# First pair's decay rows made in SBUF, small routing work of early batches on GpSimd, and a new table of planner weights in an attention + MoE + MLP kernel

## The chip, the cores and the metric

One core of one Trainium2 chip runs the whole program. Its engines are TensorE (PE in the profile, with its weight loads apart as PEld), VectorE (DVE), ScalarE (ACT), GpSimd (POOL) and SyncE (SP), which here only issues DMAs. The metric is the device time of one execution in microseconds; lower is better.

## The reference, cut to what matters

```python
def _attn_ref(q, k, v, f):                 # (4, 8, 576, 64), f (4, 8, 576)
    scores = scale * np.matmul(q, k.transpose(0, 1, 3, 2))
    cum = np.cumsum(np.log(np.clip(f, 0.0001, 1.0)), axis=-1)
    decay = cum[:, :, :, None] - cum[:, :, None, :]
    scores = np.where(causal, -1000000000.0, scores + decay)
    scores = scores - np.max(scores, axis=-1, keepdims=True)
    attn = np.exp(scores)
    attn = attn / (np.sum(attn, axis=-1, keepdims=True) + 1e-09)
    return np.matmul(attn, v)

def _moe_ref(x, w_gate, w_output_gate, w1, w2):   # x (2304, 512), 8 experts
    logits = x @ w_gate
    e_idx = np.argmax(logits, axis=1)
    probs = softmax(logits); gate_w = probs[np.arange(N), e_idx]
    eom = 1.0 / (1.0 + np.exp(-(x @ w_output_gate)))
    out[mask] = gate_w[mask, None] * eom[mask, e, None] * (np.maximum(x[mask] @ w1[e], 0) @ w2[e])

def _moe2_ref(x, w_in, w_out, a, b):              # a rational activation between two matmuls
    h = x @ w_in
    g = (a0 + a1*h + a2*h**2 + a3*h**3) / (1 + |b0|*|h| + |b1|*h**2 + 1e-06)
    return g @ w_out
```

## The kernel before, in words

The program has four stages: attention with its routing (0 to about 200 us), the token routing (to about 216 us), the experts (to about 480 us) and the last MLP. The change is in the first two.

Attention works on 16 pairs of heads (`pair(p)`, four pairs to a batch of 576 tokens). For one pair, K and Q come by DMA (`rk`, `rq`) and are split into a high and a low float32r part: `kh` (a cast on VectorE) and `qs` (ScalarE), then `kl`, the low half of `qs`, and a copy `q2s`. These three run on GpSimd for pairs 1 to 15 and on VectorE for pair 0. `kls` and `q2s` also hold two spare rows per head: `q2s` has ones there, and `kls` the cumulated log decay of the keys (a high and a low part), so that the second of the two score matmuls (L457) adds the decay. `kls`, `q2s` and `qs` have two buffers each, blanked by memsets at the start.

The decay itself is made once for all 32 heads at the start: `f` is loaded to 32 partitions, clipped, put through Ln, summed by a scan, split into high (`f_high`, L329) and low (`f_low`, L333), and stored to a scratch tensor `cum_d` in DRAM (L338, two DMAs). Each pair's `load_c` (L388) reads its four rows from there into `kls`.

A pair's scores are then taken in seven steps (the tiles of 128 queries, some for both heads at once). A step is two score matmuls per head (L456 and L457; L467 and L468 for the last 64 queries of both heads), a masked minimum on VectorE (`least`, L479 and L491), the exponential on ScalarE (L511, L522), transposes on TensorE (L598, L578, L582), and the copy of the transposed weights out of PSUM (`move`, L291 on ScalarE or L293 on VectorE). When a pair's weights are there, PV (L621) follows, and its result is copied to `ot`.

After a batch's four pairs, `batch(b)` routes its tokens: the sums of the weights (`tails`, `swap`, `tails2`, `norm`), logits from `ot` (`logit`, `tr`, `scale`), the choice of the expert (`choose`), its gate (`gates_a`, `gates_x`, `gates_b`), and the token rows scaled by the factor `rg` and stored to `x_d` (`rows_t`, `rows_m`, `rows_d`). All of the small tensors there (128 x 4 to 128 x 40) are worked on by VectorE, save two activations. The last batch's choice and gates are written out behind the plan, as part of the token routing, since the next stage waits for them.

The order of everything in attention is set by a planner (`Plan`): each operation has a due time (`when`), an engine or two with a length, and what it needs, takes and frees. A list scheduler goes through them by engine and emits the instructions in that order, and no scheduler changes it afterwards (`manual_schedule`). The due times are built from one table of weights:

```python
T_STEP = (0.003, 0.167, 0.576, 1.046, 0.372, 0.855, 1.261)
...
T_BATCH, T_BATCHJ, T_ROWS = 0.299, 0.239, -5.772
```

What goes to GpSimd before the plan (the memsets, masks, constants) stands in program order with the compiler's scheduler. 80 idle matmuls (`idle`, L353) run on TensorE at the start while it has no work.

Of the kernel before, what the change touches and what calls it, by code (L numbers as in the profile page):

```python
# [21 lines left out]
P = 128  # L22
BIG = 1.0e30
# [114 lines left out]
def tile_attention_moe_mlp(  # L138
# [37 lines left out]
    nc.scalar.preload_act_table_set("natural_log_exp_and_others")  # L176

# [11 lines left out]

    identf = const.tile([P, P], F32, name="identf")  # L190
    make_identity(nc, identf)
# [20 lines left out]
    pref = ec.tile([P, NE], F32, name="pref")  # L212
    nc.gpsimd.iota(pref, pattern=[[-1, NE]], base=NE, channel_multiplier=0, allow_small_or_imprecise_dtypes=True)

    prefs = ec.tile([P, NI, NE], F32, name="prefs")
    nc.gpsimd.tensor_copy(prefs, pref.unsqueeze(1).to_broadcast([P, NI, NE]))
    nc.gpsimd.memset(prefs[TL:, NQ], 0.0)


    with ExitStack() as actx, ExitStack() as rctx:  # L220
# [8 lines left out]

        qs = [wk.tile([P, 2, S + P], F32R, name=f"qs{i}", bufs=1) for i in range(2)]  # L230
        for t in qs:
            nc.gpsimd.memset(t.bitcast(F32)[:, :, S:], 0.0)
        half = (slice(0, D), slice(D, P))
# [5 lines left out]
        for t, k in zip(q2s, kls):  # L239
            nc.gpsimd.memset(t.bitcast(F32), 0.0)  # L240
            nc.gpsimd.memset(k.bitcast(F32), 0.0)
            for h in range(2):
                nc.gpsimd.memset(t.bitcast(F32)[half[1 - h].start : half[1 - h].start + 2, h, 0:S], 1.0)
# [5 lines left out]
        mask = wk.tile([P, NQ * P], F32, name="mask", bufs=1)  # L249
        mask_t = wk.tile([P, S // 2], F32, name="mask_t", bufs=1)  # L250
        nc.gpsimd.memset(mask, 0.0)
        nc.gpsimd.memset(mask_t, 0.0)
        for t in [mask[:, (NQ - 1) * P :]] + [mask_t[h * TL : (h + 1) * TL, S // 2 - TL :] for h in range(2)]:
            nc.gpsimd.affine_select(
                out=t, in_=t, compare_op=ALU.is_ge, fill=BIG / SCALE, base=0, pattern=[[-1, t.shape[-1]]], channel_multiplier=1
            )
# [9 lines left out]
        T_STEP = (0.003, 0.167, 0.576, 1.046, 0.372, 0.855, 1.261)  # L266
        T_TRANS = (0.59, 0.851, 0.237, 0.235, -3.102, 0.47, -0.137)
# [29 lines left out]


        g0 = {}

        def f_load(e):
            g0["fl"] = wt("t")[:NBH]
            nc.sync.dma_start(out=g0["fl"], in_=f)
# [584 lines left out]
        with tc.manual_schedule():  # L888
            plan.emit()
# [761 lines left out]
```

## Time and profile before

| | us |
|---|---|
| three timed runs | 888.17, 889.30, 893.38 |
| median | 889.3 |
| the profiled execution | 889.93 |
| its span in the trace | 888.2 |

Over the span PE is busy 849.3 us (96%), DVE 747.9 (84%), ACT 615.6 (69%) and POOL 337.5 (38%). PE's busy time is that of pipelined matmuls, and its ends are modelled: a full PE means that it always had a matmul under way. The gap of 1.7 us between the profiled execution and its span lies ahead of and behind what the trace covers. In a timeline each line is the start, the length, the engine, the line of the kernel, the operation and tiles, and in brackets how long the engine had been idle and what ended that; in a group, the busy time and the mean length in ns stand behind the first bar.

### The profile page before, as it was taken

The page shows a single profiled execution, that of the slowest core. Times are in us where ns is not written, and L with a number is a line of the kernel's source. Part 1 is how long each engine was busy: PE and PEld are TensorE (multiplying, and loading weights), DVE is VectorE, ACT ScalarE, POOL GpSimd, SP SyncE. Part 2 cuts the span into 40 slices and gives each one's busy share as a digit, 9 for nine tenths or more (in the row PEclk, how much of TensorE's full clock was granted, in tenths as well). Part 3 has the DMA queues.
Part 4 walks back from the last instruction along what each step waited for, and adds up shares of the span by engine and source line. Part 5 has one row for each costly group of instructions (what it writes and reads, how often), then busy time and mean ns, then how long its engine had stood idle before and what let it go on. Part 6 is the DMA issues. An engine that isn't in the chain of part 4 may idle for free. (4 is left out here: it accounts for less than half of the span.)

```text
span 888.2 us, 15292 instructions
## 1 busy us (share of the span) xinstructions
PE 849.3 (96%) x4667; PEld 705.0 (79%) x4667; DVE 747.9 (84%) x1428; ACT 615.6 (69%) x1282; POOL 337.5 (38%) x364
## 2 busy tenths in 40 slices
PE   6999898996999999999999999999999999999997
PEld 6787786764888887888787788899888889988885
DVE  7798999778798878778876999898898878988882
ACT  4889897876465667567545878777676667777772
POOL 7888586502113232223241233343233224324222
PEclk9999999997999999999999999999999999999999
DMA  6776567604866588789564121010000001000001
GB/s 167 167 182 168 154 175 212 199 27 151 298 218 217 177 263 310 226 288 316 195 218 154 48 72 37 0 60 24 13 36 25 12 1 57 16 1 36 1 0 48
DMA packets 49130, 110.32 MB, mean 124 GB/s; under 512 B 8405, under 2 KB 12526, under 8 KB 49038
## 3 DMA queue, kind: packets, MB, share of 16 engines
q1 hardware_dynamic: 36910, 69.90, 26.4%
q0 software_dynamic: 12128, 39.34, 13.3%
q8 instruction: 40, 0.66, 0.3%
q14 instruction: 52, 0.43, 0.2%
HBM read 151.79 MB, written 20.35 MB: 194 GB/s over the span
## 5 line engine op out<-in xcount | busy, mean ns | idle before, releaser
L1519 POOL TENSOR_TENSOR gl<-raw,gh 128x512 fp32r<-128x512 f32 (+1 forms) x71 | 84.2, 1186 | 207.3 <-ACT gh L1517 127.2
L1535 PE MATMUL pa<-wu,gl 128*128 128x512 f32 x256 | 100.6, 393 | 1.1 <-POOL gl L1519 1.1
L1533 PE MATMUL pa<-wu,gh 128*128 128x512 f32 x256 | 101.2, 395 | 0.0
L1534 PE MATMUL pa<-wu,gh 128*128 128x512 f32 x256 | 100.1, 391 | 0.0
L1492 ACT ACTIVATE raw<-ph 128x512 f32<-128x512 f32 (+1 forms) x80 | 44.3, 554 | 78.1 <-PE ph L1484 74.8
L1058 DVE TENSOR_TENSOR wu<-raw,wu 128x1024 fp32r<-128x1024 f32 x64 | 75.2, 1219 | 8.0 <-ACT wu L1056 6.6
L511 ACT ACTIVATE pr<-t,mn 128x384 f32<-128x384 f32 (+3 forms) x128 | 70.7, 557 | 16.0 <-DVE mn L479 15.4
L1505 DVE SCALAR_TENSOR_TENSOR raw<-raw,coef,raw 128x512 f32<-128x512 f32 (+1 forms) x80 | 66.2, 827 | 17.8 <-ACT raw L1501 15.1
L1495 DVE SCALAR_TENSOR_TENSOR raw<-raw,babs 128x512 f32<-128x512 f32 (+1 forms) x80 | 58.3, 729 | 20.9 <-ACT raw L1493 20.2
L1482 PE MATMUL ph<-colAh,wi 128*128 128x512 f32 x192 | 74.9, 390 | 1.0 <-ACTq L1423 0.7
L1484 PE MATMUL ph<-colAh,wi 128*128 128x512 f32 x192 | 74.7, 389 | 0.0
L1483 PE MATMUL ph<-colAl,wi 128*128 128x512 f32 x192 | 74.7, 389 | 0.0
L1056 ACT ACTIVATE wu<-raw 128x1024 fp32r<-128x1024 f32 x64 | 63.8, 1066 | 4.1 <-DMA raw<-in_w_dram 2.2
L479 DVE CUSTOM_DVE_ANT_0 t<-s,mask 128x384 f32<-128x384 f32 (+3 forms) x128 | 57.8, 484 | 6.5 <-PE s L457 3.0
L1506 DVE SCALAR_TENSOR_TENSOR raw<-raw,cbias 128x512 f32<-128x512 f32 (+1 forms) x80 | 57.6, 720 | 2.3
L1500 ACT ACTIVATE raw<-raw,cbias 128x512 f32<-128x512 f32 (+1 forms) x80 | 55.0, 687 | 6.3 <-DVE raw L1495 5.8
L1494 ACT ACTIVATE raw<-ph,neg 128x512 f32<-128x512 f32 (+1 forms) x80 | 59.3, 741 | 0.0
L1535 PEld LDWEIGHTS pa<-wu,gl 128*128 128x128 f32 x256 | 48.0, 188 | 12.7 <-POOL gl L1519 2.4
L1497 DVE SCALAR_TENSOR_TENSOR raw<-raw,coef,ph 128x512 f32<-128x512 f32 (+1 forms) x80 | 55.5, 694 | 2.5
L1533 PEld LDWEIGHTS pa<-wu,gh 128*128 128x128 f32 x256 | 48.1, 188 | 9.5 <-ACT gh L1517 0.7
L1534 PEld LDWEIGHTS pa<-wu,gh 128*128 128x128 f32 x256 | 48.1, 188 | 9.0
L1507 DVE SCALAR_TENSOR_TENSOR raw<-raw,raw 128x512 f32<-128x512 f32 (+1 forms) x80 | 52.4, 655 | 2.4
(263 smaller groups left out, 2391.9 us busy)
## 6 DMA issues: line engine op xcount, KB each, us to landing
raw<-in_w_dram SPq DMA_DIRECT2D x92, 1024.0 KB
rk<-in_kT_dram SPq DMA_DIRECT2D x30, 288.0 KB
rq<-in_qT_dram SPq DMA_DIRECT2D x30, 288.0 KB
d<-in_w_in_dram POOLq DMA_DIRECT2D x16, 512.0 KB
d<-in_w_out_dram POOLq DMA_DIRECT2D x16, 512.0 KB
y_d<-ys SPq DMA_DIRECT2D x22, 256.0 KB
v<-in_v_dram SPq DMA_DIRECT2D x16, 256.0 KB
wo_d<-d POOLq DMA_DIRECT2D x16, 256.0 KB
```

The lines of the kernel that those rows point to most:

```text
L511: nc.scalar.activation(u["pr"][:, sl], u["t"][:, sl], AF.Exp, bias=u["mn"][:, m : m + 1], scale=-1.0, accum_out=sm[:, i, 2 * hp + h : 2 * ...
L1056: nc.scalar.activation(w[:, 0], r, AF.Copy)
L1058: nc.vector.tensor_tensor(w[:, 1], r, w[:, 0].bitcast(F32), ALU.subtract)
L1482: nc.tensor.matmul(out_, wh, hi[:, :, c], start=(c == 0), stop=False)
L1483: nc.tensor.matmul(out_, wh, lo[:, :, c], start=False, stop=False)
L1484: nc.tensor.matmul(out_, wl_, hi[:, :, c], start=False, stop=(c == KD - 1))
L1494: nc.scalar.activation(u_, ph, AF.Identity, scale=neg[:, 3:4], bias=neg[:, 2:3])
L1505: nc.vector.scalar_tensor_tensor(u_, u_, coef[:, 0:1], rr, ALU.subtract, ALU.mult)
L1519: low.tensor_tensor(d["gl"], d["u_"], d["gh"].bitcast(F32), ALU.subtract)
L1533: nc.tensor.matmul(a_, gh[:, sl], wh, start=(m == 0), stop=False)
L1534: nc.tensor.matmul(a_, gh[:, sl], wl_, start=False, stop=False)
L1535: nc.tensor.matmul(a_, gl[:, sl], wh, start=False, stop=(m == MF - 1))
```

## The change

- The first pair's two decay rows per head are made in SBUF. `f` is loaded to 66 partitions, so that the first batch's heads 0 and 1 also lie on the partitions that pair 0's `kls` needs; clip, Ln, scan and `f_high` work on 66 partitions, with a column `sgn` as the factor, and `f_rows` writes the rows straight to `kls` (two operations of 2 x 576 on VectorE). Pair 0's `load_c` is gone. The other pairs still read `cum_d`; its two stores and the 32-row `f_low` are due later. The loads of `f` are three DMAs (two on SyncE's queue, one on ScalarE's), and the activation table is preloaded behind ScalarE's.
- Pair 0's second `kh` and its two `q2s` copies go from VectorE to ScalarE, and its `kls` memset from GpSimd to VectorE. The memsets and masks are reordered, with what pair 0 needs first; `identf`, `pref` and `prefs` come later, and the loads of `coef` are planned into SyncE's queue behind the second pair.
- In batches 0 to 2, the sums, products and differences of small tensors whose operands are all in SBUF go to GpSimd (12 operations a batch: `tt`, `sums`, `ex`, `gs`, `den`, `oz`, `rg`), and each is planned as an operation of its own. Reductions, reciprocals and what reads PSUM stay on VectorE. The choice takes the first maximum from the difference `ex` in one operation in place of two. The last batch uses the same functions on VectorE.
- The table of weights is new throughout.

```diff
-    nc.scalar.preload_act_table_set("natural_log_exp_and_others")
...
+    sgn = ec.tile([P, 2], F32, name="sgn")
+    nc.vector.memset(sgn, 1.0 / SCALE)
+    for r in (0, D):
+        nc.vector.memset(sgn[r : r + 1, 0:1], -1.0 / SCALE)
+        nc.vector.memset(sgn[r : r + 1, 1:2], 0.0)
...
+
+        def blank(i, on):
+            t = q2s[i].bitcast(F32)
+            on.memset(kls[i].bitcast(F32), 0.0)
+            nc.gpsimd.memset(t, 0.0)
             for h in range(2):
-                nc.gpsimd.memset(t.bitcast(F32)[half[1 - h].start : half[1 - h].start + 2, h, 0:S], 1.0)
+                nc.gpsimd.memset(t[half[1 - h].start : half[1 - h].start + 2, h, 0:S], 1.0)
+            nc.gpsimd.memset(qs[i].bitcast(F32)[:, :, S:], 0.0)
+
+        blank(0, nc.vector)
...
+        T_STEP = (-0.667, 0.087, 0.246, 0.842, 0.232, 0.882, 0.93)
...
+        T_BATCH, T_BATCHJ, T_ROWS = 0.558, 0.17, 1.464
...
+            g0["fl"] = wt("t")
+            nc.scalar.dma_start(out=g0["fl"][D:NF], in_=f[0:1, :].to_broadcast([2, S]))
+            nc.sync.dma_start(out=g0["fl"][F0], in_=f)
+            nc.sync.dma_start(out=g0["fl"][0:NBH], in_=f[1:2, :].to_broadcast([NBH, S]))
+            nc.scalar.preload_act_table_set("natural_log_exp_and_others")
...
         def f_high(e):
-            g0["ch"] = wt("pr")[:NBH].bitcast(F32R)
-            nc.scalar.activation(g0["ch"], g0["cum"], AF.Copy, scale=1.0 / SCALE)
+            g0["ch"] = wt("pr").bitcast(F32R)
+            nc.scalar.activation(g0["ch"][:NF], g0["cum"][:NF], AF.Copy, scale=sgn[:NF, 0:1])
...
+        def low_of(rows, to):
+            nc.vector.scalar_tensor_tensor(
+                to, g0["cum"][rows], sgn[rows, 1:2], g0["ch"][rows].bitcast(F32), ALU.mult, ALU.subtract
+            )
+
+        def f_rows(h):
+            r = half[1 - h].start
+            return lambda e: low_of(slice(r, r + 2), kls[0][r : r + 2, h, :])
...
+            g0["cl"] = wt("pr").bitcast(F32R)
+            low_of(F0, g0["cl"][F0])
...
-        o_cl = plan.op(early, {"DVE": 669}, f_low, [o_ch], takes=["pr"], frees=[("t", o_cum)])
+        o_first = [plan.op(early, {"DVE": 669}, f_rows(0), [o_ch], takes=["c"])]
+        o_first.append(plan.op(-1.2 * SPAN, {"DVE": 669}, f_rows(1), [o_ch]))
+        o_cl = plan.op(-1.1 * SPAN, {"DVE": 669}, f_low, [o_ch], takes=["pr"], frees=[("t", o_cum)])
...
+            plan.op(-0.9 * SPAN, {"SP": 650}, f_store(0, "ch"), [o_ch], frees=[("pr", o_ch)]),
+            plan.op(-0.9 * SPAN, {"SP": 650}, f_store(1, "cl"), [o_cl], frees=[("pr", o_cl)]),
...
-            l_c = plan.op(tl + 0.3 * SPAN, {"SP": 1200}, load_c, o_cst, takes=["c"])
+            l_c = plan.op(tl + 0.3 * SPAN, {"SP": 1200}, load_c, o_cst, takes=["c"]) if p else o_first[0]
+            l_cs = [l_c, l_c] if p else o_first
...
+                    evac(e, d["kh"][:, h], d["rk"][:, h])
...
+                        nc.scalar.activation(to, x, AF.Copy)
...
-                o_kh.append(plan.op(w, {"DVE": 420}, kh(h), [lk[h]] + o_kh[:1], takes=["kh"] if h == 0 else []))
+                o_kh.append(plan.op(w, {"DVE": 420} if p or h == 0 else {"ACT": 620}, kh(h), [lk[h]] + o_kh[:1], takes=["kh"] if h == 0 else []))
...
+                q2e = {"POOL": 1340} if p else {"ACT": 620}
...
+                    if p == 0 and si < 2:
+                        (o_first[1], o_cl)[si].needs.append(o_l_)
...
+            on, ON = (nc.vector, "DVE") if b == B - 1 else (nc.gpsimd, "POOL")
...
                     def tails(e):
-                        nc.vector.tensor_tensor(g["tt"], g["tsum"][:, 0, :], g["tsum"][:, 1, :], ALU.add)
+                        on.tensor_tensor(g["tt"], g["tsum"][:, 0, :], g["tsum"][:, 1, :], ALU.add)
+                        on.tensor_copy(tails_of()[:, :, 0], g["tt"][:TL])
...
+                        nc.vector.tensor_copy(tails_of()[:, :, 1], g["pn"][:TL, :NHP])
...
+                    a = plan.op(wn(), {ON: 400}, tails, (sums_done or ready) + [o_mk])
...
+                def plus(e, some=some):
+                    for r, sl in some:
+                        on.tensor_scalar_add(g["sums"][r, sl, :], g["sums"][r, sl, :], 1.0e-9)
...
+                        nc.vector.reciprocal(g["rc"][r, sl, :], g["sums"][r, sl, :])
...
+                o_n = plan.op(wn(), {ON: 200 * len(some)}, plus, need + (sums_done or ready) + [o_mk])
+                o_n = plan.op(wn(), {"DVE": 230 * len(some)}, norm, [o_n])
...
-                nc.vector.tensor_tensor(sc, lg, g["lmax"].unsqueeze(2).to_broadcast(SH), ALU.is_equal)
-                nc.vector.tensor_tensor(sc, sc, prefs, ALU.mult)
...
+            def first(e=None):
+                nc.vector.scalar_tensor_tensor(g["sc"][:, :, 0:NE], g["ex"], 0.0, prefs, ALU.is_equal, ALU.mult)
...
+            def from_top(e=None):
+                on.tensor_tensor(g["ex"], *logits(), ALU.subtract)
+
+            def own_gate(e=None):
+                on.tensor_tensor(g["gs"], g["lgb"][:, :, NE : 2 * NE], ohb, ALU.mult)
...
-                nc.vector.tensor_reduce(den, g["ex"], AX.X, ALU.add)
+                on.tensor_scalar_add(den, den, 1.0e-9)
+                if b < B - 1:
+                    on.tensor_scalar_add(g["oz"], g["oz"], 1.0)
+                    on.tensor_tensor(den, g["oz"], den, ALU.mult)
+                else:
+                    yield
+                    on.scalar_tensor_tensor(den, g["oz"], 1.0, den, ALU.add, ALU.mult)
...
+            def den_rc(e=None):
+                nc.vector.reciprocal(g["den"], g["den"])
+
+            def factors():
                 for r in ((slice(0, P), slice(0, NQ)), (slice(0, TL), slice(NQ, NI))):
...
                         g["rg"][r[0], r[1], :], g["rc"][r[0], r[1], :],
...
+                        g["den"][r[0], r[1]].unsqueeze(2).to_broadcast([r[0].stop, r[1].stop - r[1].start, H]), ALU.mult,
...
-            o = plan.op(wn(), {"DVE": 1000}, choose, prev_red)
-            o = plan.op(wn(), {"DVE": 350}, gates_a, [o])
-            o = plan.op(wn(), {"ACT": 230}, gates_x, [o])
-            o_g = plan.op(wn(), {"DVE": 650}, lambda e: deque(gates_b(), 0), [o])
...
+            o = plan.op(wn(), {"DVE": 230}, top, prev_red)
+            o = plan.op(wn(), {"POOL": 250}, from_top, [o])
+            o = plan.op(wn(), {"DVE": 850}, both(first, first_max, chosen), [o])
+            o_x = plan.op(wn(), {"ACT": 230}, exps, [o])
+            o = plan.op(wn(), {"POOL": 250}, own_gate, [o])
+            o_d = plan.op(wn(), {"DVE": 230}, exp_sum, [o_x])
+            o = plan.op(wn(), {"DVE": 230}, gate_sum, [o])
+            o = plan.op(wn(), {"ACT": 200}, gate_exp, [o])
+            o = plan.op(wn(), {"POOL": 500}, through(den_all), [o, o_d])
+            o = plan.op(wn(), {"DVE": 220}, den_rc, [o])
+            o_g = plan.op(wn(), {"POOL": 400}, through(factors), [o])
...
+        plan.op(2 * SPAN, {"SP": 1300}, load_coef, [st[1]["o_ot"]])
```

Of 2341 instructions that VectorE issued (its rows counted singly) 2316 are left, and GpSimd has 36 more compute operations. From the last batch's gates on, every engine's order is the one of before.

SyncE's DMA queue behind the first loads of K and Q (`rk`, `rq` 64 x 576 are pair 0's, 64 x 1152 pair 1's; `v` the values). Before:

```order
L338 DMA cum_d<-pr 32x576
L374 DMA rq<-in_qT_dram 64x576 x2
L902 DMA coef<-in_ca_dram 128x4
L903 DMA coef<-in_cb_dram 128x2
L338 DMA cum_d<-pr 32x576
L382 DMA v_129<-in_v_dram 128x2x256
L383 DMA v_129<-in_vt_dram 64x2x64
L388 DMA kl_119<-cum_d 2x576 x2
L374 DMA rk<-in_kT_dram 64x1152 x2
L374 DMA rq<-in_qT_dram 64x1152 x2
```

and after:

```order
L407 DMA rq<-in_qT_dram 64x576 x2
L415 DMA v_142<-in_v_dram 128x2x256
L416 DMA v_142<-in_vt_dram 64x2x64
L407 DMA rk<-in_kT_dram 64x1152 x2
L407 DMA rq<-in_qT_dram 64x1152 x2
L369 DMA cum_d<-pr 32x576 x2
L415 DMA v_143<-in_v_dram 128x2x256
L416 DMA v_143<-in_vt_dram 64x2x64
L421 DMA kl_113<-cum_d 2x576 x2
```

Pair 1's loads have moved ahead of both stores of `cum_d`, and pair 0's read of it is gone.

VectorE from its first work on `f` to the first `least` (ISA rows). Before:

```order
L322 TENSOR_SCALAR t<-t 32x576
L315 SCALAR_TENSOR_TENSOR t<-pr 32x576
L411 CAST kh<-rk 128x576
L416 TENSOR_TENSOR kl_119<-rk,kh 64x576
L333 SCALAR_TENSOR_TENSOR pr<-t,pr 32x576
L425 TENSOR_TENSOR qs_113<-rq,qs_113 64x576
L430 TENSOR_SCALAR q2s_117<-rq 64x576
L411 CAST kh<-rk 128x576
L416 TENSOR_TENSOR kl_119<-rk,kh 64x576
L430 TENSOR_SCALAR q2s_117<-rq 64x576
L425 TENSOR_TENSOR qs_113<-rq,qs_113 64x576
L479 ISA t,mn<-s,mask 128x384
```

and after:

```order
L331 TENSOR_SCALAR t<-t 66x576
L339 SCALAR_TENSOR_TENSOR t<-pr 66x576
L306 CAST kh<-rk 128x576
L450 TENSOR_TENSOR kl_112<-rk,kh 64x576
L356 SCALAR_TENSOR_TENSOR kl_112<-t,sgn,pr 2x576
L459 TENSOR_TENSOR qs_108<-rq,qs_108 64x576
L450 TENSOR_TENSOR kl_112<-rk,kh 64x576
L517 ISA t,mn<-s,mask 128x384
```

The decay rows are written between the first head's `kl` and `qs`, and both `q2s` copies, one cast and the second head's `qs` no longer stand ahead of the first minimum.

VectorE at the gates of the second batch (`den` the denominator, `rg` the factor). Before:

```order
L411 CAST kh<-rk 128x576
L771 TENSOR_REDUCE den<-ex 128x5
L773 TENSOR_SCALAR den<-den 128x5
L775 SCALAR_TENSOR_TENSOR den<-oz,den 128x5
L777 RECIPROCAL den<-den 128x5
L780 TENSOR_TENSOR rg<-rc,den 128x32
L780 TENSOR_TENSOR rg<-rc,den 64x8
L479 ISA t,mn<-s,mask 128x384
```

and after, where the reciprocal stands (its `den` is now made on GpSimd, among the `kl` and `qs` work of the coming pairs):

```order
L517 ISA t,mn<-s,mask 128x384
L517 ISA mn 128x1
L840 RECIPROCAL den<-den 128x5
L529 ISA t,mn<-s,mask 128x288
L529 ISA mn 128x1
```

The chain of six is broken up: VectorE's reduction stands 28 rows ahead of the reciprocal, with minima and copies between, and the sums and products are not in its queue.

## Rows read from the trace of the kernel before

**Rows 1.** Stretches of 20 us: length, busy PE, PEld, DVE, ACT, POOL, clock, DMA, GB/s.

```profile
120.00:140.00 20.00, 20.00 (x165) 16.66 (x164) 18.08 (x66) 17.55 (x58) 15.28 (x16) 1.00 0.88 232
140.00:160.00 20.00, 15.94 (x125) 13.10 (x123) 19.49 (x52) 14.55 (x46) 11.58 (x12) 1.00 0.70 196
...
200.00:220.00 20.00, 11.40 (x80) 8.72 (x80) 17.07 (x51) 13.82 (x38) 6.36 (x6) 0.74 0.43 135
220.00:240.00 20.00, 20.00 (x103) 16.54 (x103) 15.10 (x34) 8.14 (x15) 3.31 (x4) 1.00 0.94 327
```

**Rows 2.** Timeline, SyncE's DMA queue in the first 14 us.

```profile
0.82 0.41 SPq L303 DMA_DIRECT2D t<-in_f_dram  x1
...
8.73 0.36 SPq L338 DMA_DIRECT2D cum_d<-pr  x1
...
12.06 0.58 SPq L388 DMA_DIRECT2D kl<-cum_d  x2
...
12.69 1.13 SPq L374 DMA_DIRECT2D rk<-in_kT_dram  x2
```

**Rows 3.** Timeline, the engines from 1 us to 27 us.

```profile
1.96 7.04 PE L353 MATMUL po<-after,onesb 128*128 128x128 bf16 x80 [1.96 <-POOL onesb L200]
...
2.75 0.45 DVE L322 TENSOR_SCALAR t<-t 32x576 f32<-32x576 f32 x1 [1.22 <-DMA t<-in_f_dram]
...
3.95 1.35 DVE L315 TENSOR_TENSOR_SCAN t<-pr 32x576 f32<-32x576 f32 x1 [0.75 <-ACT pr L311]
4.36 1.05 POOL L241 MEMSET kl<- 128x1152 f32 x1
5.22 0.50 DVE L411 CAST kh<-rk 128x576 fp32r<-128x576 f32 x1
5.33 0.68 ACT L329 ACTIVATE pr<-t 32x576 fp32r<-32x576 f32 x1 [1.41 <-DVE t L315]
...
6.51 0.74 DVE L333 SCALAR_TENSOR_TENSOR pr<-t,pr 32x576 fp32r<-32x576 f32 x1
...
7.28 0.76 DVE L425 TENSOR_TENSOR qs<-rq,qs 64x576 fp32r<-64x576 f32 x1
...
13.57 0.41 PE L457 MATMUL s<-kl,q2s 128*128 128x384 f32 x1 [4.35 <-DMA kl<-cum_d]
...
21.37 1.25 ACT L422 ACTIVATE qs<-rq 128x576 fp32r<-128x576 f32 x2 [1.08 <-DMA rq<-in_qT_dram]
...
26.27 0.56 DVE L479 CUSTOM_DVE_ANT_0 t<-s,mask 128x384 f32<-128x384 f32 x1 [1.44 <-PE s L457]
```

**Rows 4.** Busy time and granted clock of a short stretch, columns as in rows 1.

```profile
14.00:17.00 3.00, 3.00 (x12) 2.80 (x12) 2.19 (x8) 2.10 (x6) 1.66 (x13) 0.50 0.96 247
```

**Rows 5.** Waits of TensorE from 9 to 207 us: total us, times, longest.

```profile
PE s L467 <- DVE mn L479: 4.8, 2, 2.6
```

**Rows 6.** Timeline around the second batch's gates.

```profile
140.82 1.41 POOL L416 TENSOR_TENSOR kl<-rk,kh 64x576 fp32r<-64x576 f32 x1 [3.54 <-DVE kh L411]
...
140.87 1.39 DVE L773 TENSOR_SCALAR den<-den 128x5 f32<-128x5 f32 x1
...
142.36 1.36 DVE L775 SCALAR_TENSOR_TENSOR den<-oz,den 128x5 f32<-128x5 f32 x1
```

**Rows 7.** VectorE's groups by shape, 55 to 192 us.

```profile
L681 DVE TENSOR_TENSOR tt<-tsum 128x4 f32<-128x4 f32 x4 | 3.1, 769 | 0.0
L775 DVE SCALAR_TENSOR_TENSOR den<-oz,den 128x5 f32<-128x5 f32 x3 | 2.7, 907 | 0.3
...
L780 DVE TENSOR_TENSOR rg<-rc,den 128x32 f32<-128x32 f32 x3 | 1.6, 541 | 0.1
```

**Rows 8.** One line's instructions over the whole span: shortest, median, longest.

```profile
L773 DVE TENSOR_SCALAR den<-den x4: 171/172/1387, 96.4 to 202.4; 128x5 f32<-128x5 f32 x4
```

**Rows 9.** Timeline: a small GpSimd operation, and a late store.

```profile
14.29 0.29 POOL L929 TENSOR_SCALAR s<-s 128x25 f32<-128x25 f32 x1
...
164.58 0.68 DVE L796 TENSOR_TENSOR xr<-pt,rg 64x512 f32<-64x512 f32 x1 [2.91 <-DMA x_d<-xr]
```

More of the change, by code (lines that the diff above doesn't have):

```diff
@@ L227, in tile_attention_moe_mlp, with edge @@
         ps_o = actx.enter_context(tc.tile_pool(name="ps_o", bufs=2, space=PSUM))
+        half = (slice(0, D), slice(D, P))
         qs = [wk.tile([P, 2, S + P], F32R, name=f"qs{i}", bufs=1) for i in range(2)]
-        for t in qs:
-            nc.gpsimd.memset(t.bitcast(F32)[:, :, S:], 0.0)
-        half = (slice(0, D), slice(D, P))
         q2s = [wk.tile([P, 2, S + P], F32R, name=f"q2s{i}", bufs=1) for i in range(2)]
         kls = [ld.tile([P, 2, S], F32R, name=f"kl{i}", bufs=1) for i in range(2)]
-        for t, k in zip(q2s, kls):
-            nc.gpsimd.memset(t.bitcast(F32), 0.0)
-            nc.gpsimd.memset(k.bitcast(F32), 0.0)
+        def blank(i, on):
+            t = q2s[i].bitcast(F32)
+            on.memset(kls[i].bitcast(F32), 0.0)
+            nc.gpsimd.memset(t, 0.0)
             for h in range(2):
-                nc.gpsimd.memset(t.bitcast(F32)[half[1 - h].start : half[1 - h].start + 2, h, 0:S], 1.0)
+                nc.gpsimd.memset(t[half[1 - h].start : half[1 - h].start + 2, h, 0:S], 1.0)
+            nc.gpsimd.memset(qs[i].bitcast(F32)[:, :, S:], 0.0)
+        blank(0, nc.vector)
+        mask = wk.tile([P, NQ * P], F32, name="mask", bufs=1)
+        mask_t = wk.tile([P, S // 2], F32, name="mask_t", bufs=1)
+        def edge(t):
+            nc.gpsimd.affine_select(
+                out=t, in_=t, compare_op=ALU.is_ge, fill=BIG / SCALE, base=0, pattern=[[-1, t.shape[-1]]], channel_multiplier=1
+            )
+        nc.gpsimd.memset(mask, 0.0)
+        edge(mask[:, (NQ - 1) * P :])
+        identf = const.tile([P, P], F32, name="identf")
+        make_identity(nc, identf)
+        nc.gpsimd.memset(mask_t, 0.0)
+        for h in range(2):
+            edge(mask_t[h * TL : (h + 1) * TL, S // 2 - TL :])
+        blank(1, nc.gpsimd)
         vs = [ld.tile([P, 2, NI, D], F32, name=f"v{i}", bufs=1) for i in range(3)]
@@ L247, in tile_attention_moe_mlp @@
             nc.gpsimd.memset(t[: P - TL, :, NQ], 0.0)
[L249 to L256, printed above, removed]
+        pref = ec.tile([P, NE], F32, name="pref")
+        nc.gpsimd.iota(pref, pattern=[[-1, NE]], base=NE, channel_multiplier=0, allow_small_or_imprecise_dtypes=True)
+        prefs = ec.tile([P, NI, NE], F32, name="prefs")
+        nc.gpsimd.tensor_copy(prefs, pref.unsqueeze(1).to_broadcast([P, NI, NE]))
+        nc.gpsimd.memset(prefs[TL:, NQ], 0.0)
         CUT = NQ // 2
@@ L783, in gates_b, with choose, gates_a, gates_x @@
                     )
                     yield
+            def choose():
+                for step in (top, from_top, first, first_max, chosen):
+                    step()
+            def gates_a():
+                for step in (own_gate, gate_sum):
+                    step()
+            def gates_x():
+                exps()
+                gate_exp()
+            def gates_b():
+                exp_sum()
+                yield
+                yield from den_all()
+                den_rc()
+                yield
+                yield from factors()
```

124 lines of the change are left out of this document (54 added, 70 removed).

## Prediction

> **What bounds the kernel now.** I read the busy time by stretches first, then the timeline of the start, the waits of TensorE, and the timeline around the longest of them.
>
> The stretches say which part can move. From 220 us on TensorE is busy 20.00 of 20 us [rows 1], and no instruction behind the last batch's gates changes its place, so what the change is worth is decided before about 200 us and is handed on to the end unchanged. In attention itself there are two kinds of stretch. From 120 to 140 us TensorE is full while VectorE has 18.08 and ScalarE 17.55 us [rows 1]: there TensorE is the bound, and time taken from another engine gives nothing. From 140 to 160 us TensorE has 15.94 us and VectorE 19.49 [rows 1]: there TensorE waits. So the gain must come from where TensorE stands still, and such places are few.
>
> The first is the start. Its idle matmuls run from 1.96 us for 7.04 us, to 9.0; the first L457, which adds the decay, starts at 13.57 after 4.35 us of waiting for the DMA that brings pair 0's decay rows back from DRAM [rows 3]. The reader is to see the way of that data: f is there at 2.75, clip, Ln and scan end at 5.30, the high part at 6.01 and the low part at 7.25 [rows 3], the low part's store is issued at 8.73, the read at 12.06 [rows 2]. From 7.25 to 13.57 nothing is computed on it; it is only carried.
>
> The second kind are two waits of TensorE for a minimum, 4.8 us together [rows 5]. The timeline shows the second one's cause: in the second batch's gates two operations on 128 x 5 numbers take 1.39 and 1.36 us, each begun just after a GpSimd operation of 1.41 us on SBUF [rows 6], where the same line takes 0.171 us otherwise [rows 8]. The minima stand behind them in VectorE's queue.
>
> **The start.** Two effects shift the chain. Ahead of the clip VectorE now has the memset of pair 0's kls, 1.05 us on GpSimd's row [rows 3], a memset of half that width and five small ones, some 2 us from its first instruction at 1.0; and the third load of f delays SyncE's K and Q by one issue of 0.41 [rows 2]. Clip at 3.2 in place of 2.75, then. Clip to scan takes the same 2.55 us (the width is 576 on any number of partitions), to 5.75; the high part 0.68 more, to 6.45. Meanwhile VectorE does the first cast (0.50) and its kl (as long as the other subtraction, 0.76), to 7.0; the decay rows cost what the low part costs, 0.74, to 7.75; the low half of qs 0.76, to 8.5 [rows 3]. The q2s copy runs beside that on ScalarE. So scores can start at about 8.7, and the idle matmuls end at 9.0: 13.57 - 9.0 = 4.5 us. It would be 2.5 if GpSimd's memsets held up both the clip and the cast by 1.05 each, and 5 if the idle matmuls were the only bound.
>
> Will the second pair follow? Its q waits for its load until 21.37, and its first minimum comes at 26.27 [rows 3]. That load was behind the read of cum_d in SyncE's queue, issued from 12.69 [rows 2]. Now it comes behind two issues of f, four pairs of loads at 1.13 and the two of v: 0.82 + 0.82 + 4.5 + 1.2 = 7.4 us, up to 8. So pair 1 is moved up by about as much as pair 0, and I let 4.5 stand. The stores of cum_d now stand behind pair 1's loads, and pair 1's own decay rows behind them; SyncE waits there for the low part, which VectorE writes behind two minima (about 12 us), and what is queued behind it is v of pair 1 and K and Q of pair 2, issued near 15 where they had been issued at about 17 to 19.
>
> A smaller term: from 14 to 17 us the granted clock is 0.50, TensorE's lower level of 1.2 GHz, after the wait; TensorE is busy all 3.0 us [rows 4]. Without the 4.35 us of standing still I expect the scores at 2.4 GHz. That is at most 1.5 us, and VectorE's 2.19 of 3.0 us lies beside it; I take 0.4.
>
> **The gates of batches 0 to 2.** Twelve operations a batch leave VectorE. The three largest groups alone hold 3.1 + 2.7 + 1.6 us [rows 7], where operations of 0.17 would hold less than 2; most of what goes is waiting. Where TensorE is full this is worth nothing, as above. At the two stalls it is worth 4.8 us: the long operations of the second (1.39 + 1.36, less 0.34 that they need) are 2.4 us, against a stall of 2.6. One operation takes the place of two in the choice, and its two inputs are both in SBUF, so it can be held once more for up to 1.4; the reciprocals and reductions that stay are the 0.2 us ones. Against it stand the handovers: in a batch VectorE takes five results from GpSimd (two sums before reciprocals, ex, gs, den), and each can be late by the GpSimd operation ahead of it, 1.41 [rows 6]. The order puts minima and copies between (28 rows from the reduction to the reciprocal), so I charge 0.5 us in all and take 4.3 for this part; its bounds are 0 and 4.8.
>
> On GpSimd the twelve cost about 0.29 each [rows 9], 3.5 us a batch. It had 4.7 us free from 120 to 140 and 8.4 from 140 to 160 [rows 1], which covers them over the 40 to 45 us of a batch; if that cover were gone, a pair's inputs would come 3.5 us later, in three batches.
>
> A collision shows as a small operation on VectorE that lasts as long as the GpSimd operation beside it [rows 6]. The Trainium skill (SBUF — State Buffer, "Who interferes with whom") states it as a lock: a VectorE operation with two SBUF inputs, or in a two-port mode, and a GpSimd operation that reads SBUF exclude each other for the whole instruction, and issue order decides who waits. The trace agrees. By that rule the change does not end collisions: the casts stay, and twelve more GpSimd operations a batch may hold VectorE. That case is the third rival, worked out below from rows.
>
> **The rest.** In the last batch the choice and gates have one operation less on the way to the routing, 0.2 us [rows 8]. The load of coef, the constants and the preloaded table move to places where nobody waits: 0. The new weights reorder all of attention. Full stretches can't win; the worst stretch has 4.1 us of idle TensorE, of which 2.6 is the stall counted above, so a stretch is worth about 1.5 us either way: 0, with that as its bound, once a batch. A store that VectorE's row scaling waited 2.91 us for [rows 9] may stay.
>
> Sum: 4.5 + 0.4 + 4.3 + 0.2 = 9.4 us. The profiled execution took 889.93 us (span 888.2, 1.7 around it), which would become 880.5; it stands 0.6 above the median of the runs, 889.3, and for that I say **880**.
>
> **Rivals.** First: VectorE waits for GpSimd in place of being held by it. Fifteen handovers, each behind a kl or qs operation of 1.41 us, are 21 us of VectorE's time, and the second stall shows that such time reaches TensorE whole: 889.9 - 4.5 - 0.4 - 4.8 - 0.2 + 21 = 901. From 0.65 us a handover the change gains nothing (9.9 / 15), from 1.25 it is slower by over 1%. For it: GpSimd works in order and is busy 15.28 of 20 us where TensorE is full [rows 1]. Against it: the distance in VectorE's order. 6%.
>
> Second: the start is not handed on. The DMA engines are busy 0.96 from 14 to 17 us [rows 4]; if pair 1's Q lands no earlier than its bandwidth allows, or the clip and cast are held, pair 0's lead becomes a wait at pair 1. Gain there 0 to 1.5: about 884. Against it: from 8.73 to 12.06 SyncE mostly stood waiting [rows 2], and these bytes now start earlier. 13%.
>
> Third: the start is won, but in the batches new collisions (casts, the merged choice, the late store) take the place of the old: about 885. 17%.
>
> Fourth: VectorE's relief, some 4 us a batch, also ends the losses behind the stalls (the stretch from 140 to 160 lost 4.1 us, 1.5 more than the stall) and the start gains 5: 875. 14%.
>
> **How the numbers follow.** The forecast has 50%. About 1% is what a measurement of this kernel can tell from no change, 8.9 us, so the forecast of 9.3 lies at that edge: some three fifths of its cases are beyond it. Faster by over 1%: 0.30 from it, 0.14 from the fourth, 0.04 from the second and third: 0.48. Within 1%: 0.46. Slower: 0.06, the first rival. The range leaves out the first rival and the ends of the third and fourth: 872.5 (start 5, clock 1.5, stalls 4.8, 1.5 in each of three batches and another 1 for the store) to 887.5 (start 2.5 and the batches nothing, with 0.7 lost).
>
> **What will show it.** The first L457 at about 9 us with no wait for cum_d, and the granted clock at 1.00 from 9 to 20. Pair 1's first minimum near 21.5 in place of 26.3. No operation of 128 x 5 on VectorE over 0.4 us in the first three batches, and no wait of TensorE's L467 for a minimum (L479) of over 2 us. If VectorE's idle time names GpSimd's ex, gs, den or sums, the first rival is at work; if TensorE is idle between pairs 0 and 1 for DMA, the second. I would be wrong as a whole if the new table made stretches like 120 to 140 us less than full.

## The result and the profile after

The changed kernel takes 882.91 us (median of 7 runs, 879.36 to 883.66), the kernel before 891.29 us beside it (888.17 to 895.99): a ratio of 0.9896 with a 95% interval of 0.9874 to 0.9919, 1.04% faster. 880 had been forecast. The profiled executions differ by 10.5 us (889.93 and 879.41); the changed kernel's is its second fastest of seven, 3.5 us under the median. Times of single rows below come from such executions, verdicts from the ratios.

Stretches of the changed kernel, columns as in [rows 1]:

```profile
120.00:140.00 20.00, 20.00 (x162) 16.50 (x161) 19.52 (x67) 17.51 (x57) 16.35 (x19) 1.00 0.70 189
140.00:160.00 20.00, 19.50 (x171) 15.29 (x168) 17.54 (x57) 16.71 (x53) 15.94 (x23) 1.00 0.99 277
200.00:220.00 20.00, 17.98 (x101) 14.25 (x102) 16.23 (x38) 9.57 (x14) 8.53 (x8) 0.89 0.68 215
220.00:240.00 20.00, 20.00 (x100) 16.56 (x99) 15.50 (x29) 11.98 (x19) 2.24 (x4) 1.00 0.73 249
14.00:17.00 3.00, 2.88 (x20) 2.72 (x20) 2.37 (x9) 1.21 (x3) 2.83 (x7) 1.00 0.77 203
```

From 140 to 160 us TensorE is busy 19.50 us where it had 15.94 [rows 1], though the changed kernel is then some us further on in its work; from 120 to 140 it is full, as before. The last line answers to [rows 4]: the granted clock is 1.00, 2.4 GHz, where it had been 0.50.

The start in the timeline of the changed kernel, against [rows 3]:

```profile
3.02 1.19 POOL L237 MEMSET q2s<- 2x576 f32 x2
3.60 1.40 DVE L331 TENSOR_SCALAR t<-t 66x576 f32<-66x576 f32 x1 [0.61 <-DMA t<-in_f_dram]
4.16 0.51 POOL L250 MEMSET mask<- 128x512 f32 x1
...
5.74 1.36 DVE L339 TENSOR_TENSOR_SCAN t<-pr 66x576 f32<-66x576 f32 x1 [0.75 <-ACT pr L335]
...
7.13 0.78 ACT L353 ACTIVATE pr<-t,sgn 66x576 fp32r<-66x576 f32 x1 [1.42 <-DVE t L339]
...
8.27 0.81 DVE L356 SCALAR_TENSOR_TENSOR kl<-t,sgn,pr 2x576 fp32r<-2x576 f32 x1
...
9.00 0.74 DVE L459 TENSOR_TENSOR qs<-rq,qs 64x576 fp32r<-64x576 f32 x1
...
10.08 0.33 PE L495 MATMUL s<-kl,q2s 128*128 128x384 f32 x1
...
14.01 0.44 DVE L306 CAST kh<-rk 128x576 fp32r<-128x576 f32 x1
...
16.39 0.69 ACT L456 ACTIVATE qs<-rq 128x576 fp32r<-128x576 f32 x1 [1.73 <-DMA rq<-in_qT_dram]
...
20.15 0.55 DVE L517 CUSTOM_DVE_ANT_0 t<-s,mask 128x384 f32<-128x384 f32 x1
```

L495 (L457 before) starts at 10.08 in place of 13.57 and waits for no DMA. Its chain would be a microsecond shorter but for the clip: 1.40 us where it had 0.45. (In `same_order_on_VectorE` below, with the same start, the clip took 0.50 us, and the first minimum came at 9.49 in place of 10.57.) Pair 1's first minimum is at 20.15 in place of 26.27.

TensorE's waits from 9 to 207 us in the changed kernel, columns as in [rows 5], the four longest groups:

```profile
PE pid L1126 <- DVE op__3313 L1121: 7.1, 4, 5.9
PE pt L638 <- ACT pr L549: 2.9, 5, 0.9
PE pt L638 <- DVE pT L306: 2.3, 4, 1.1
PE s L494 <- DVE qs L459: 1.6, 1, 1.6
```

The first is routing, behind attention. No wait for a minimum is left, and no single one in attention is longer than 1.6 us. The small operations of the first three batches stand on GpSimd now (its groups from 50 to 192 us; the second number is the mean in ns, behind the bar is the idle time ahead and who ended it):

```profile
L811 POOL TENSOR_TENSOR ex<-lgb,lmax 128x40 f32<-128x40 f32 x3 | 1.1, 357 | 5.7 <-DVE lmax L799 5.5
L724 POOL TENSOR_TENSOR tt<-tsum 128x4 f32<-128x4 f32 x3 | 1.0, 318 | 0.2
L814 POOL TENSOR_TENSOR gs<-lgb,oh 128x40 f32<-128x40 f32 x3 | 0.9, 293 | 4.6 <-DVE oh L808 4.6
L830 POOL TENSOR_SCALAR den<-den 128x5 f32<-128x5 f32 x3 | 0.7, 245 | 2.4 <-DVE den L826 2.3
```

`tt` takes 318 ns where VectorE's mean had been 769 [rows 7]. The idle times say who pays for the handovers: GpSimd waits for VectorE, 12.4 us in these three groups, and VectorE waits for GpSimd in one place (1.2 us, for `den`).

### The profile page after: what moved, and what is told of

The parts are those of the page before. It is cut to its first block, busy times and chain, and to the rows that moved or that the text cites. A ratio compares the mean times of both kernels' runs of the same rounds, so it can differ in the third digit from the quotient of the medians.

```text
span 877.7 us, 15315 instructions
## 1 busy us (share of the span) xinstructions
PE 846.6 (96%) x4667; PEld 702.0 (80%) x4667; DVE 734.3 (84%) x1403; ACT 616.5 (70%) x1278; POOL 347.0 (40%) x399
```

## The experiments

Each ratio is to the kernel before on the same chip. "Last PV" is where the last matmul of attention's output (L621, L661 after) starts in the profiled execution. The rows were measured in four groups, in which the kernel before had medians of 891.29 to 893.28 us, so ratios are to be compared between rows and not medians. The last PV is that of one execution each, and the changed kernel's 183.5 comes from a fast one. From the last PV to its end a profiled execution took 695.9 us (before, changed) to 701.6 (`gates_and_weights`), so a ratio does not follow the last PV exactly.

| kernel | median us | ratio, 95% interval | last PV, us |
|---|---|---|---|
| before | 891.29 | 1 | 194.0 |
| changed | 882.91 | 0.9896 (0.9874 to 0.9919) | 183.5 |
| start_and_weights | 896.38 | 1.0045 (1.0024 to 1.0066) | 199.3 |
| gates_and_weights | 898.21 | 1.0071 (1.0034 to 1.0109) | 197.8 |
| start_and_gates | 895.27 | 1.0036 (1.0012 to 1.0059) | 198.3 |
| same_order_on_VectorE | 891.75 | 1.0003 (0.9979 to 1.0026) | 191.6 |
| start_later | 884.22 | 0.9911 (0.9885 to 0.9938) | 185.5 |
| clip_of_two_inputs | 882.22 | 0.9878 (0.9856 to 0.99) | 184.3 |
| weights_2_percent_up | 887.07 | 0.9933 (0.9908 to 0.9958) | 191.8 |
| before_weights_2_percent_up | 896.18 | 1.0038 (1.0019 to 1.0057) | 198.2 |
| start_own_weights | 888.13 | 0.9933 (0.9905 to 0.9961) | 189.6 |
| gates_own_weights | 883.05 | 0.9886 (0.9863 to 0.9909) | 188.2 |
| both_other_weights | 891.49 | 0.9979 (0.996 to 0.9999) | 193.5 |
| gates_moved_unplanned | 885.55 | 0.993 (0.9906 to 0.9953) | 191.7 |

My theory was the forecast's: a start worth some 4 us and gates worth some 4, with weights that are neutral. The rival: the new weights, an order chosen for this list of operations, carry the gain.

**One part left out at a time.** In `start_and_weights` the gates' code is that of before, in `gates_and_weights` the start's; in `start_and_gates` only the table is old. One line of each:

```diff
-            o = plan.op(wn(), {"DVE": 230}, top, prev_red)
-            o = plan.op(wn(), {"POOL": 250}, from_top, [o])
...
+            o = plan.op(wn(), {"DVE": 1000}, choose, prev_red)
```

```diff
-            l_c = plan.op(tl + 0.3 * SPAN, {"SP": 1200}, load_c, o_cst, takes=["c"]) if p else o_first[0]
+            l_c = plan.op(tl + 0.3 * SPAN, {"SP": 1200}, load_c, o_cst, takes=["c"])
```

```diff
-        T_STEP = (-0.667, 0.087, 0.246, 0.842, 0.232, 0.882, 0.93)
+        T_STEP = (0.003, 0.167, 0.576, 1.046, 0.372, 0.855, 1.261)
...
-        T_BATCH, T_BATCHJ, T_ROWS = 0.558, 0.17, 1.464
+        T_BATCH, T_BATCHJ, T_ROWS = 0.299, 0.239, -5.772
```

> The changed kernel with its gates of batches 0 to 2 back as they were (all on VectorE, planned in four steps), start and weights new. If the gain is a sum of a start and of gates, as predicted: first L457 near 10.1 us and pair 1's first minimum near 20.2 as in the changed kernel, operations of 128x5 that last over 0.9 us on VectorE again, waits of TensorE for minima of about 5 us in all, end of attention (last L621) 4 to 5 us later than the 183.8 us of the changed kernel: 188, and a time of about 0.995 of before. If the weights carry the gain: end of attention near 184 and 0.990, whatever engine has the gates. If the weights fit only the steps that they were chosen for: 190 or later, and 1.000 or worse.

> The changed kernel with the start of before (decay rows through DRAM), gates and weights new. If the gain is a sum: first L457 near 13.6, pair 1's first minimum near 26.3, no wait of TensorE for a minimum over 2 us, end of attention at about 188 (183.8 and the 4.1 us of work by which the changed kernel led at 40 us), time 0.995 of before. If the start is not handed on and all of the gain is from the batches: end near 184 and 0.990. If the order that the weights make is what counts, the two starts give different orders and the end lies anywhere from 186 to 194.

> The changed kernel with the old table of weights: start and gates new. By the forecast, which gave the weights 0 with a bound of 1.5 us a batch: end of attention 184 to 187, time 0.989 to 0.994 of before. If the weights are needed to keep VectorE from waiting for GpSimd's small results: waits of VectorE that name GpSimd's ex, gs, den or sums of 5 us or more, end of attention 189 or later, 0.997 or worse.

All three are slower than the kernel before, by 0.4 to 0.7%. The first and the third came out as their last case had it; `gates_and_weights` ended later than any of its cases, and 5.7 us of what its profiled execution lost lie behind attention; why is open. In `start_and_gates` VectorE's waits that name GpSimd are 3.8 us, less than the 5 expected for that case, and 4.9 us wait for a store. A table serves the list of operations that it was chosen for; whatever is taken out, the rest is worth less than nothing. So these three can't price a part, and they end the forecast's 0 for the weights.

**The gates, in the same order.** GpSimd's small operations go back to VectorE, planned as before, so that TensorE's and ScalarE's orders stay what they are:

```diff
-            on, ON = (nc.vector, "DVE") if b == B - 1 else (nc.gpsimd, "POOL")
+            on, ON = nc.vector, "DVE" if b == B - 1 else "POOL"
```

> The changed kernel in the same order on every engine, but the small products, sums and differences of batches 0 to 2 are issued on VectorE where GpSimd had them. If collisions with GpSimd were what the old gates cost: among the 39 operations that come back several last 0.9 to 1.4 us, VectorE has 10 to 20 us more work and waiting from 50 to 192 us, TensorE stalls behind it and attention ends 2 to 5 us later than at 183.8; time 0.993 to 0.996 of before. If it was the order (minima no longer right behind the gates): operations of 0.2 to 0.3 us, or long ones that nobody waits for, end of attention within 0.7 us of 183.8, and 0.990.

The whole gain goes, 1.0003: more than collisions had been given (0.993 to 0.996). TensorE's waits for minima are back in this kernel (9 to 207 us), 5.6 us together:

```profile
PE s L505 <- DVE mn L517: 4.2, 5, 1.5
...
PE s L494 <- DVE mn L517: 1.4, 3, 0.6
```

and its timeline shows a collision. `ex` came back from GpSimd; L802 is on VectorE in the changed kernel too:

```profile
93.83 0.27 DVE L811 TENSOR_TENSOR ex<-lgb,lmax 128x40 f32<-128x40 f32 x1
94.11 1.42 POOL L459 TENSOR_TENSOR qs<-rq,qs 64x576 fp32r<-64x576 f32 x1
94.13 1.46 DVE L802 SCALAR_TENSOR_TENSOR sc<-ex,prefs 128x40 f32<-128x40 f32 x1
...
95.62 0.20 DVE L805 TENSOR_REDUCE smax<-sc 128x5 f32<-128x45 f32 x1
...
96.25 0.72 DVE L517 CUSTOM_DVE_ANT_0 t<-s,mask 128x512 f32<-128x512 f32 x1
...
97.04 0.40 PE L505 MATMUL s<-kh,qs 128*128 128x288 f32 x1 [1.51 <-DVE mn L517]
```

L802 reads two inputs in SBUF, begins 0.02 us behind GpSimd's `qs` and ends with it: 1.46 us for an operation whose mean in the changed kernel is 0.196. The reduction behind it is not held. The next minimum stands behind these operations, and TensorE waits 1.51 us for it. This is the lock that the forecast cited from the Trainium skill (SBUF — State Buffer, "Who interferes with whom"), and the trace agrees: the two-input form and GpSimd's reading operation, one at a time. VectorE's work in five groups here (50 to 192 us) is 3.1 us for L802, 2.1 for `gs`, 1.9 for `tt`, 1.7 and 1.0 for `rg`:

```profile
L802 DVE SCALAR_TENSOR_TENSOR sc<-ex,prefs 128x40 f32<-128x40 f32 x3 | 3.1, 1017 | 0.1
L814 DVE TENSOR_TENSOR gs<-lgb,oh 128x40 f32<-128x40 f32 x3 | 2.1, 706 | 0.0
```

There is a rival that this run does not rule out: that VectorE has more work, held or not. The operations that come back are 36 (12 a batch; the expectation counts 39). By their groups in this window they take VectorE 11.4 us, of which about 6 would be left if each took its shortest time; L802 and L808, which stayed on VectorE, take 3.0 us more than in the changed kernel. So about 8 us is holding and about 6 plain work, an estimate from these groups. No run takes off the one without the other, so what the collisions alone cost is not measured.

**The gates alone, without planning.** The kernel before, its start, table and plan untouched; the same products, sums and differences of batches 0 to 2 issued on GpSimd where VectorE had them:

```diff
             cnt = [0]
+            on = nc.vector if b == B - 1 else nc.gpsimd
...
-                        nc.vector.tensor_tensor(g["tt"], g["tsum"][:, 0, :], g["tsum"][:, 1, :], ALU.add)
+                        on.tensor_tensor(g["tt"], g["tsum"][:, 0, :], g["tsum"][:, 1, :], ALU.add)
...
-                nc.vector.tensor_tensor(g["ex"], lg, g["lmax"].unsqueeze(2).to_broadcast(SH), ALU.subtract)
+                on.tensor_tensor(g["ex"], lg, g["lmax"].unsqueeze(2).to_broadcast(SH), ALU.subtract)
```

> The kernel before with the same small operations of batches 0 to 2 issued on GpSimd, in the places where VectorE had them, and planned as if VectorE still did them. This is the first rival made real: the reciprocals and reductions stand right behind the results they need. If a handover waits for the kl or qs operation ahead of it (1.41 us): VectorE waits for GpSimd's sums, ex, gs, den for 10 to 20 us in all from 50 to 192 us, last PV at 198 to 210, 1.005 to 1.018 of before. If handovers are short (0.3 to 0.5 us): the stalls on minima shrink and the end is at 190 to 195, 0.996 to 1.001.

0.993, faster than either expectation: 6.2 us of 893, from where the operations stand alone. TensorE's two waits for a minimum at L467 [rows 5] are gone from its list (9 to 207 us). The forecast had read the cause of the second only; the trace of the kernel before shows the same for the first, held operations beside GpSimd's `kl` and `qs` (96.41 to 99.33 us) and the minimum behind them:

```profile
96.68 1.20 DVE L775 SCALAR_TENSOR_TENSOR den<-oz,den 128x5 f32<-128x5 f32 x1
...
98.14 1.31 DVE L780 TENSOR_TENSOR rg<-rc,den 128x32 f32<-128x32 f32 x2
...
99.98 0.40 PE L467 MATMUL s<-kh,qs 128*128 128x288 f32 x1 [2.23 <-DVE mn L479]
```

VectorE's waits for GpSimd in this kernel from 50 to 192 us:

```profile
DVE den L782 <- POOL den L778: 3.0, 3, 1.0
...
DVE rc L701 <- POOL sums L700: 1.2, 3, 0.7
```

4.2 us of the 21 that the first rival had, though nothing was planned singly. The rival counted a `kl` or `qs` of 1.41 us ahead of each handover. The trace shows GpSimd already standing at the operation when its input comes: it is idle 7.7 us ahead of `ex` and 5.5 ahead of the first `den` for want of VectorE's result, as in the changed kernel's 5.7 and 4.6 us above. A first handover puts GpSimd in step with VectorE, and the price is GpSimd's idle time, for which it had room.

**The start, in the same order.** Three scans of zeros ahead of the scan of f:

```diff
             g0["cum"] = wt("t")
+            z = g0["zf"][:NF]; [nc.vector.tensor_tensor_scan(out=z, data0=z, data1=z, initial=0.0, op0=ALU.add, op1=ALU.add) for _ in range(3)]
```

> The changed kernel in its order, with three more scans of zeros on VectorE ahead of the scan of f: 3 x 1.36 us, less the 0.75 us that VectorE waits there for Ln, so the decay rows and the first minimum come 3.3 us later (13.9 in place of 10.57), as late as in the kernel before within 0.3. If the start is handed on to the end, as predicted (4.5 us): pair 1's first minimum 3 us later, end of attention 186.5 to 187.5 in place of 183.8, time 0.993 to 0.994 of before. If the loads or GpSimd's work for pair 1 set the pace by then: end of attention within 1 us of 183.8 and 0.990 to 0.991, and the gain of the start came from pair 1's early loads alone.

Timeline of VectorE:

```profile
3.39 0.51 DVE L331 TENSOR_SCALAR t<-t 66x576 f32<-66x576 f32 x1 [0.40 <-DMA t<-in_f_dram]
...
12.93 0.56 DVE L518 CUSTOM_DVE_ANT_0 t<-s,mask 128x384 f32<-128x384 f32 x1 [0.22 <-PE s L496]
```

The clip was not held here, so the first minimum came 2.4 us later, not 3.3; pair 1's came 3.3 later (23.49), the last PV 2.0, and the ratio is 0.0015 higher (1.3 us). As far as one execution of each can show, the start is handed on in part: a delay that puts back two thirds of the lead over the kernel before (12.93 against 14.14 there) costs 2 us of attention. But the executions of the changed kernel differ by up to 4.3 us among themselves, and 0.9911 can't be told from 0.9896, so the share handed on is not settled.

**The clip.** The held operation in another form, its second input a column of ones:

```diff
-            nc.vector.tensor_scalar(x, x, 1.0e-4, 1.0, op0=ALU.max, op1=ALU.min)
+            nc.vector.scalar_tensor_tensor(x, x, 1.0e-4, sgn[:NF, 2:3].to_broadcast([NF, S]), ALU.max, ALU.min)
```

> The changed kernel in its order, with the clip as one operation of two inputs (the second a column of ones) in place of the one-input operation that took 1.40 us beside GpSimd's memsets. If memsets hold only the one-input form: 0.7 to 0.75 us, first L494 at 9.1 to 9.2 in place of 9.80, end of attention up to 0.7 us earlier, 0.988 to 0.990 of before. If memsets hold any operation of VectorE there, or the width of 66 partitions is what costs: 1.4 us again and no difference. If q's load is what the first scores wait for by then: clip shorter, first L494 no earlier than 9.5.

Timeline, the clip beside the same memsets, and pair 1's first cast:

```profile
3.02 1.19 POOL L237 MEMSET q2s<- 2x576 f32 x2
3.47 0.76 DVE L331 SCALAR_TENSOR_TENSOR t<-t,sgn 66x576 f32<-66x576 f32 x1 [0.46 <-DMA t<-in_f_dram]
4.16 0.51 POOL L250 MEMSET mask<- 128x512 f32 x1
...
14.49 0.56 DVE L306 CAST kh<-rk 128x576 fp32r<-128x576 f32 x1 [1.18 <-DMA rk<-in_kT_dram]
```

0.76 us, and the first scores at 9.03, as expected of memsets that hold only the one-input form. Nor does the clip hold them: they keep 1.19 us, where the one-input clip that came first stretched them to 1.40 (last section). But pair 1's cast now waits for K until 14.49, its first minimum is at 21.07, the last PV comes 0.8 us later where up to 0.7 earlier was expected, and the time is the same within the intervals. What is won at the clip ends at pair 1's load: second rival, for this microsecond.

**The weights.** Every number of the table times 1.02, in the changed kernel and in the one before:

```diff
-        T_BATCH, T_BATCHJ, T_ROWS = 0.558, 0.17, 1.464
+        T_BATCH, T_BATCHJ, T_ROWS = 0.5692, 0.1734, 1.4933
```

> The changed kernel with each number of the table of weights times 1.02: the same work and the same planner, a slightly other order in attention. By the forecast's bound for an order (1.5 us a batch either way, so about 3 for three) : end of attention 182 to 187, 0.987 to 0.994 of before. If the table is chosen for this very list of operations, and orders nearby lose what it found: end at 188 or later, 0.995 or worse, with TensorE's waits spread over copies, exponentials and minima in place of one cause.

> The kernel before with each number of its own table times 1.02. If its order was as good as its operations allow, as the one beside it is: later than 194.0 at the end of attention by 2 to 10 us, 1.002 to 1.011 of before. If orders nearby are worth the same: 192 to 196, 0.998 to 1.002.

A step of 2% upward costs 0.37% (0.9933 against 0.9896; the two intervals still touch) and 0.38%. For the changed kernel the time fits the first case and the last PV (191.8) the second. Both tables stand at a good place as far as this one direction shows.

**Parts with tables of their own.** The three mixtures of the first group, each with a table searched for its own list; the last line of each table, in the order of the expectations, against the changed kernel's:

```diff
-        T_BATCH, T_BATCHJ, T_ROWS = 0.558, 0.17, 1.464
+        T_BATCH, T_BATCHJ, T_ROWS = 0.515, 0.209, 37.463
+        T_BATCH, T_BATCHJ, T_ROWS = 1.1, 0.168, 34.745
+        T_BATCH, T_BATCHJ, T_ROWS = 0.072, 0.178, 3.443
```

> The new start with the gates of before (all on VectorE), and a table of weights searched for this list of operations until the planner's own sum of its lengths ends attention at 181.3 us (183.4 for the kernel before, 184.9 for the changed kernel). If the gates on VectorE are what keeps the chip behind its plan (before: last PV at 194.0 against 183.4 planned): 8 to 11 us over the plan, last PV at 189 to 192, time 0.995 to 0.998 of before, operations of 128x5 over 0.9 us on VectorE. If any searched table does what the changed kernel's does: 184 or sooner, 0.990 or better. If a searched table fails on the chip for other reasons: 195 or later.

> The start of before with the new gates, and a table searched for this list until the planner's own sum ends attention at 184.9 us. If gates on GpSimd, planned singly, keep the chip at its plan (changed kernel: last PV at 183.4 against 184.9 planned): last PV at 184 to 188, time 0.990 to 0.995 of before, so that the gates alone bring 6 us or more and the start 2 to 3. If the gain needs both parts: 190 or later, 0.997 or more.

> The changed kernel with another table, searched from the old one until the planner's own sum ends attention at 183.7 us (184.9 with the kernel's own). If a table that is good by the plan is good on the chip once the gates are on GpSimd: last PV at 181 to 187, 0.986 to 0.994 of before. If the kernel's own table has something that the plan doesn't count: 189 or later, 0.996 or worse; then the waits of VectorE for GpSimd's results or for loads tell what.

The gates with the old start, 0.9886, are as fast as the change as a whole; the start with the old gates has 0.9933; both with another table 0.9979. The first two are faster than the cases that their last PVs come nearest to; the third is its second case. The planner's own sums, given in the expectations, do not rank the tables: 184.9 us for `gates_own_weights` (last PV at 188.2), 181.3 for `start_own_weights` (189.6), 183.7 for the other table (193.5) and 184.9 for the changed kernel's own (183.5). The kernel before was not given a newly searched table, and no run has the new start alone in the order of before, so what of 0.9886 and 0.9933 the search brought is not shown. The last one's waits, VectorE's and then TensorE's:

```profile
DVE xr L880 <- DMA x_d<-xr: 6.9, 3, 5.3
```

```profile
PE pt L618 <- DVE xr L880: 5.0, 1, 5.0
```

The row scaling (`xr`) of the second batch waits for a store to free its buffer, and TensorE stands behind it. `start_own_weights` has the same, 4.4 us and 4.0 behind it; the kernel before had 2.91 [rows 9]; the changed kernel has none. `gates_moved_unplanned` has 3.7 us of it with only 0.5 us of TensorE's behind it, so such a wait does not always cost. That this wait is what the other table lost is read from the profile; no run tried it by itself.

## Why the prediction was right, and where it was not

**The size held, and both mechanisms show in the traces.** 9.4 us were forecast, 10.5 came in the profiled executions and 8.4 in the medians. Behind 200 us nothing changed but the time at which it began (the last PV 10.5 us earlier). That the terms add up to this is in part luck, as the weights below show.

**Start, 4.5 forecast.** The wait for cum_d is gone; L457 moved by 3.5. The step that failed is "Clip at 3.2 ... Clip to scan takes the same 2.55 us": the clip began at 3.60, and from there to the end of the scan it took 3.50, since the clip was held (the forecast had that case in its lower bound, 2.5). The lead at pair 1 is 6.1, more than forecast, as the loads of pair 1 moved ahead of the stores. Handed on to the end it seems less than "I let 4.5 stand": `start_later` lost 2.0 us of attention for 3.3 at pair 1, so 6.1 there would be 3.7, an estimate by that share, which rests on one execution each. With `clip_of_two_inputs` this makes the second rival look partly true.

**Clock, 0.4 forecast.** The granted clock is 1.00 from 14 to 17 us, as forecast. Its price was not measured apart.

**Gates, 4.3 forecast.** The mechanism, held operations on VectorE with minima behind them, is shown from both sides, in the traces and in the times: moved alone, 6.2 us (0.47% to 0.94% of 893, 4.2 to 8.4); taken back in the changed kernel's order, 9.6 us. How much of this is holding and how much plain work is not separated. The 4.3 lies just inside the first interval; against the second it is too small, and mis-sized is "worth 4.8 us" at the two stalls. It may be that where stretches are not full VectorE's relief also counts behind other waits, which no run tried by itself; that was the fourth rival's mechanism, whose 875 us didn't come. The 0.5 us for handovers was too small, 1.2 us on VectorE, but little beside the rival's 21.

**Weights, 0 forecast, with "about 1.5 us either way" once a batch.** The term that failed most. On one list of operations four tables gave 0.9896, 0.9933, 0.9979 and 1.0036 of before: 12.5 us between the ends, where three batches had been given 4.5 either way. I had bounded an order by the worst stretch that the trace of before showed, but that trace shows one good order; a bad one makes waits that it doesn't contain, such as 5.3 us for a store. The forecast came out because the table delivered with the change is a good one for it, which the profile before could not tell: in this the forecast was lucky. How that table was chosen is not on record.

**Rivals.** The first, 21 us of handovers, fell: 1.2 us measured, 4.2 without planning. The third, new collisions, did not show: L808 and L802 stand at 0.340 and 0.196 us in the changed kernel, and the casts' mean is 0.663 us (0.660 before, 50 to 192 us). The parts don't add up: gates alone with a table of their own reach what both reach. Whether the start brings anything beside well-planned gates stays open within 0.3%.

## What to carry to other kernels

Small operations on VectorE beside long GpSimd operations can cost far more than their length, those with two inputs (1.46 us for 0.196 here) and one-input sums too (1.39 for 0.171 [rows 6, rows 8]); look for groups whose mean is several times their shortest, and try moving them to the engine that they collide with; here that paid even unplanned (0.993). Where a planner's table sets the order, an edit and its table are one change: price an edit with the other engines' orders held fixed; here the table alone moved the time by 0.4 to 1.4%. A microsecond won at the start counts only as far as the second tile's loads move with it: the one won at the clip ended at pair 1's K.

## What the hardware showed that I had not expected

A memset on GpSimd, which reads nothing, holds a one-input operation on VectorE, and which of the two comes first turns on hundredths of a us. In the new start the clip, which waits for f, begins at 3.37 to 3.42 us in four of the profiles and takes 0.50 to 0.55, with GpSimd's memsets at 1.40 in place of 1.19; in four others it begins at 3.58 to 3.68 and takes 1.32 to 1.42. In the old start, 2.75 gave 0.45 [rows 3], and 2.80 gave this, from the timeline of `gates_moved_unplanned`:

```profile
2.80 2.65 DVE L322 TENSOR_SCALAR t<-t 32x576 f32<-32x576 f32 x1 [1.28 <-DMA t<-in_f_dram]
2.87 1.28 POOL L240 MEMSET q2s<- 128x1408 f32 x1
4.08 1.06 POOL L241 MEMSET kl<- 128x1152 f32 x1
5.20 0.77 POOL L243 MEMSET q2s<- 2x576 f32 x1
```

The clip waits through two memsets, not one. Its row begins 0.07 us ahead of the first one's, so the start of a row is not the moment that decides. The first minimum came 2.5 us later than in the kernel before (16.64 against 14.14). The profile of `gates_own_weights` has the same (2.82, 2.63 us), so the first minimum of these two profiles stands some 2.5 us later than their code alone makes it; what of that reaches their last PV was not measured. Both executions are slower than their kernel's median (888.0 against 885.55, 884.99 against 883.05). The Trainium skill (SBUF — State Buffer, "Who interferes with whom") has both halves of it: a `tensor_scalar` in a two-port mode excludes GpSimd altogether, a two-input operation only GpSimd's reads. The two-input clip agrees: 0.76 us beside the memsets of the new start, and these at their 1.19.
